# Attention with P on the array's columns: division once per head, two pairs with keys on partitions, scores by halves

## The chip, the cores and the metric

The kernel runs on one core of one Trainium2 chip. The core has a matrix engine (PE; PEld is its loading of the stationary operand, the weights), a vector engine (DVE), a scalar engine (ACT), a third elementwise engine (POOL), and a sync engine (SP), which here issues every DMA. SBUF is the on-chip working memory with 128 partitions; PSUM takes the results of matmuls in eight banks. The metric is the device time of one execution in microseconds. It is the median of several runs.

## The reference

Attention over 4 batches and 8 heads, 768 rows, 64 columns per head. A query sees only those keys that have the same six hash bits (the signs of six projections). The result of all heads goes through a gated MLP that also mixes along the sequence.

```python
q_bits = (einsum('bhsd,dk->bhsk', q, proj) > 0)      # 6 bits; the same for k
mask = q_bucket[:, :, :, None] == k_bucket[:, :, None, :]
scores = where(mask, q @ k.T / sqrt(64), -1e9)
scores = scores - max(scores, axis=-1)
attn = exp(scores); attn = attn / (sum(attn, axis=-1) + 1e-9)
x = concat_heads(attn @ v)                           # (4, 768, 512)
h = maximum(x @ w_in, 0); u, v = h[..., :512], h[..., 512:]
v_n = (v - mean(v)) / sqrt(var(v) + 1e-6)
v_s = einsum('ts,bsd->btd', w_spatial, v_n) + b_spatial[None, :, None]
out = (u * v_s) @ w_out
```

All inputs are float32. A row whose mask leaves no key at all gets the plain mean of v, because all its scores are equal.

## The kernel before, in words

**Numbers.** Every operand of a matmul is kept as two float16 parts, high and low, whose sum is the float32 value. A product is three matmuls: high times high, high times low, low times high. ACT usually makes the high part (a copy to float16), and DVE or POOL makes the low part (float32 minus high part).

**Pairs and rounds.** Two heads make a pair p (16 pairs, 4 per batch); head e of a pair sits on partitions 64e to 64e+63. A round is one block of 128 query rows of a pair, for both heads. There are six rounds per pair. In a round, `scores` does this:

- PE: for each head, 8 matmuls of 384 columns into two PSUM banks `sp` (three for the split product, one for the hash bits, whose large products push masked keys far down, for each half of the 768 keys). The two heads run on the two halves of the array's rows.
- DVE (L359): copies 128x768 scores to SBUF (`ex`), cuts them from below and takes each row's maximum (`mx`).
- POOL (L362): maximum times a negative factor (`nb`). ACT (L367): exp in place with bias `nb`, and the row sums (`sm`). POOL and DVE (L369, L370): the reciprocal `ri`.
- ACT (L373): high part of exp times `ri`. DVE (L375): the low part. Both lie in `pp`.
- SP: a transposing DMA turns `pp` into `pt`, with the keys on the partitions.

After three rounds, `weighted` multiplies: v (`vp`, high and low) is the stationary operand with 64 columns, `pt` streams 384 columns, and the two heads fill the two halves of the array's columns (36 matmuls into `pv`). The result is already the transposed attention output `xt`; ACT and DVE split it (L402, L405).

**Per pair.** SP loads k and q (`qk`) and v (`v32`); a hash product `hp` gives the signs (`sg`), which eight DMAs spread into `hr`; ACT and DVE split k and q (`hl`) and v (`vp`).

**MLP.** When the four pairs of a batch are done, `mlp` makes 28 units of PE work: six `v_unit` (vps), eight `u_unit` (ups), eight `s_unit` (sps, the mix along the sequence), six `o_unit` (ops, the output). Around them stand evacuations from PSUM, the normalisation, the gating product (POOL, `sy`) and splits of `vn` and `g` (ACT high, POOL low). In the order of the code a half batch is u, s, o.

**Weights.** `job` loads a piece of a weight matrix, brings the float64 words to float32 where needed (five small operations, four on DVE), and splits it: high on ACT, a second scaled copy on ACT, low on POOL.

**What sets the order.** All operations are recorded first with an engine, a cost and a key (the round in which they are due). `plan()` simulates the five engines with these costs, buffer rings and waits; whenever an engine is free, the ready operation with the smallest key goes next. The kernel is then written out in that order, and every engine executes its instructions strictly in it. So the costs, keys and ring sizes decide the order on each queue.

Of the kernel before, what the change touches and what calls it, by code (L numbers as in the profile page):

```python
# [6 lines left out]

F16 = mybir.dt.float16
F32 = mybir.dt.float32
I64 = mybir.dt.int64  # L10
U32 = mybir.dt.uint32
AF = mybir.ActivationFunctionType
ALU = mybir.AluOpType

P = 128
D = 64
# [7 lines left out]
SP = 16384.0  # L24
# [8 lines left out]
def lsh_attention_spatial_gating(  # L33
# [33 lines left out]


# [4 lines left out]
    for i, t in enumerate(hr):  # L73
        (nc.vector if i % 2 else nc.gpsimd).memset(t, 0.0)

# [8 lines left out]
    RING = {"sc": 2, "pv": 2, "m": 2, "hr": NHR, "qk": 1, "v32": 1, "hl": 2, "vp": 2, "sg0": 1, "sg1": 2,  # L84
            "ex": 6, "pp": 4, "pt": 4, "xt": 6, "st2": 4, "st6": 4, "v32m": 4, "vy": 2, "vn": 1, "u": 1,
            "g": 1, "sy": 2, "sm3": 2, "bs": 2, "mv": 2}
# [10 lines left out]
    unit = []  # L97

    def op(eng, dur, key, fn, r=(), w=(), kind=None, land=0.0):
        o = Op()  # L100
        o.eng, o.dur, o.key, o.fn, o.kind, o.land = eng, dur, key, fn, kind, land
        o.seq, o.new, o.start, o.end = len(ops), [], None, None
        deps = set()
        for x, wr in [(x, False) for x in r] + [(x, True) for x in w]:
# [4 lines left out]
            if wr and not b.users and b.tag is not None:  # L109
                o.new.append(b)  # L110
            b.uses.append((part, wr, o))
# [10 lines left out]
    def plan():  # L122


        SEM, MODE, DMA_LAT = 0.1, 0.1, 1.6
        LATE = {"PE": 0.17, "DVE": 0.09, "ACT": 0.1, "POOL": 0.05, "SP": 0.0}
# [8 lines left out]
        dma = 0.0  # L135
# [3 lines left out]
        def release(o):  # L139
            when[o] = max([d.end + (SEM if d.eng != o.eng or d.land else 0.03) for d in o.deps], default=0.0)  # L140
            ready[o.eng].append(o)

        def room(o):
            t = 0.0
            for b in o.new:
                ring = rings[b.tag]
                need = sum(1 for x in o.new[:o.new.index(b)] if x.tag == b.tag)
# [8 lines left out]
            return t  # L156

# [5 lines left out]
        while done < len(ops):  # L163
            nxt = None
            for e in free:
                while free[e] <= now:
                    best = None
                    for o in ready[e]:
# [3 lines left out]
                        t = max(t, when[o])  # L172
                        if t > now:
                            nxt = t if nxt is None else min(nxt, t)
                        elif best is None or (o.key, o.seq) < (best.key, best.seq):
                            best = o
# [3 lines left out]
                    ready[e].remove(o)  # L180
# [3 lines left out]
                    d = o.dur  # L184
# [4 lines left out]
                    free[e] = now + d  # L189
                    o.end = now + d + LATE[e]  # L190
# [14 lines left out]
        return sorted(ops, key=lambda o: (o.start, o.seq))  # L205

# [17 lines left out]
    def weights():  # L224
        vi, vo, vs = (x.rearrange("(c p) f -> p c f", p=P) for x in (w_in, w_out, w_sp))
        n = 0
        for src, dst, cs, lo, hi, m, f, W, key, dk in (
                (vi, wi, NPAIR, F2, DF, 256, SX, Wv, 5.0, 1.9), (vi, wi, NPAIR, 0, F2, 256, SX, Wu, 20.5, 1.0),
                (vs, ws, NT, 0, S, HS, SW, Ws, 28.0, 0.5), (vo, wo, NF, 0, DM, 256, SX, Wo, 33.5, 0.5)):
# [7 lines left out]
    def job(n, src, dst, m, f, W, key):  # L237
# [8 lines left out]
        else:  # L246
# [19 lines left out]
            for k, e, d in ((0, "ACT", 0.33), (4, "DVE", 0.2), (1, "DVE", 0.2), (2, "DVE", 0.34), (3, "DVE", 0.34)):  # L266
                op(e, d, key, lambda k=k: conv(k), r=[raw], w=[wb])
        d = 0.31 if m == 256 else 0.41
        op("ACT", d, key, lambda: nc.scalar.activation(dst[0], wb.t[:, :m], AF.Copy, scale=f), r=[wb], w=[(W, n)])
        op("ACT", d, key, lambda: nc.scalar.activation(wb.t[:, :m], wb.t[:, :m], AF.Copy, scale=f), w=[wb])  # L270
        op("POOL", 0.63 if m == 256 else 0.87, key,
           lambda: nc.gpsimd.tensor_tensor(out=dst[1], in0=wb.t[:, :m], in1=dst[0], op=ALU.subtract), r=[wb], w=[(W, n)])


    KH, KL, QH, QL = range(4)
    xts = {}

    def pair(p):
# [5 lines left out]
        def hash_():  # L284
# [7 lines left out]
        op("ACT", 0.42, k0 + 0.2, lambda: nc.scalar.activation(  # L292
            tile_of(s1, wk, [P, HS], F16, f"sg1_{p}"), s0.t, AF.Copy, scale=hv[:, 1:2]), r=[s0], w=[s1])
# [14 lines left out]
        def high():  # L308
            tile_of(hl, wk, [P, 4, S], F16, f"hl{p}")
            nc.scalar.activation(part(0), qk.t, AF.Copy, scale=SQ)  # L310

        op("ACT", 1.38, k0 + 0.5, high, r=[qk], w=[hl])
        op("DVE", 1.67, k0 + 0.6, lambda: nc.vector.scalar_tensor_tensor(
            out=part(1), in0=qk.t, scalar=SQ, in1=part(0), op0=ALU.mult, op1=ALU.subtract), r=[qk], w=[hl])
# [300 lines left out]
```

## Time and profile before

The median of three runs is 727.33 us (726.72 to 727.62). The profiled execution took 725.48 us, and its span, from the first to the last instruction, is 723.7 us; the mean granted clock of PE is 0.92.

| engine | busy us | share of the span | instructions |
|---|---|---|---|
| PE | 602.5 | 83% | 4352 |
| PEld | 302.6 | 42% | 4352 |
| DVE | 528.4 | 73% | 985 |
| ACT | 507.4 | 70% | 905 |
| POOL | 200.5 | 28% | 322 |

In the rows of a profile, `L214 PE MATMUL sp<-hl 64*128 64x384 f16 x1152 | 169.3, 374 | 82.6 <-DVE ex L359 79.7` reads: line 214, matmuls from tile hl into tile sp, 64 rows and 128 columns of the array, 64 partitions by 384 elements, 1152 of them; busy 169.3 us, 374 ns for one; PE was idle 82.6 us ahead of them, of which 79.7 until DVE had finished line 359 on tile ex. All matmuls have one line, that of a helper, so they are told apart by tiles. A row of the timeline or of the chain begins with the start and the duration in us. Records of matmuls are longer than the distance between them, because matmuls overlap in the array.

### The profile page before, as it was taken

The page shows a single profiled execution, that of the slowest core. Times are in us where ns is not written, and L with a number is a line of the kernel's source. Part 1 is how long each engine was busy: PE and PEld are TensorE (multiplying, and loading weights), DVE is VectorE, ACT ScalarE, POOL GpSimd, SP SyncE. Part 2 cuts the span into 40 slices and gives each one's busy share as a digit, 9 for nine tenths or more (in the row PEclk, how much of TensorE's full clock was granted, in tenths as well). Part 3 has the DMA queues.
Part 4 walks back from the last instruction along what each step waited for, and adds up shares of the span by engine and source line. Part 5 has one row for each costly group of instructions (what it writes and reads, how often), then busy time and mean ns, then how long its engine had stood idle before and what let it go on. Part 6 is the DMA issues. An engine that isn't in the chain of part 4 may idle for free. (4 is left out here: it accounts for less than half of the span.)

```text
span 723.7 us, 12276 instructions
## 1 busy us (share of the span) xinstructions
PE 602.5 (83%) x4352; PEld 302.6 (42%) x4352; DVE 528.4 (73%) x985; ACT 507.4 (70%) x905; POOL 200.5 (28%) x322
## 2 busy tenths in 40 slices
PE   2658566658888875999899989969998999989997
PEld 0224223333444432455344545534454555445553
DVE  3869788978799889857679876985788968864100
ACT  3768577878899768856777877785768778763221
POOL 2022122233144443106014420420033502302513
PEclk9998666666999985999999999989999999999999
DMA  4677988979798779886786869779856997790011
GB/s 137 178 160 155 223 178 159 224 142 236 124 237 150 176 166 217 186 177 138 135 202 126 171 126 217 162 152 181 159 112 139 178 178 131 146 202 3 1 45 43
DMA packets 317726, 111.73 MB, mean 154 GB/s; under 512 B 304224, under 2 KB 307296, under 8 KB 317664
## 3 DMA queue, kind: packets, MB, share of 16 engines
q1 hardware_dynamic: 317664, 110.94, 74.3%
q8 instruction: 34, 0.56, 0.3%
q14 instruction: 28, 0.23, 0.1%
HBM read 27.94 MB, written 6.29 MB: 47 GB/s over the span
## 5 line engine op out<-in xcount | busy, mean ns | idle before, releaser
L214 PE MATMUL sp<-hl 64*128 64x384 f16 x1152 | 169.3, 374 | 82.6 <-DVE ex L359 79.7
L375 DVE SCALAR_TENSOR_TENSOR pp<-ex,ri,pp 128x768 f16<-128x768 f32 x192 | 199.2, 1063 | 46.9 <-ACT pp L373 46.0
L373 ACT ACTIVATE pp<-ex,ri 128x768 f16<-128x768 f32 x192 | 172.3, 927 | 56.5 <-DMA pt<-pp 21.9
L367 ACT ACTIVATE ex<-ex,nb 128x768 f32<-128x768 f32 x192 | 177.5, 925 | 42.9 <-POOL nb L362 42.8
L359 DVE TENSOR_SCALAR_CACHE_REDUCE ex<-sp 128x768 f32<-128x768 f32 x192 | 179.2, 947 | 23.6 <-PE sp L214 23.3
L214 PEld LDWEIGHTS <-hl 64*128 64x128 f16 x1152 | 66.7, 103 | 171.0 <-issue 117.8
L214 PE MATMUL pv<-pt,vp 128*64 128x384 f16 x1152 | 112.7, 350 | 10.5 <-DMA pt<-pp 10.4
L214 PE MATMUL sps<-ws,vn 128*128 128x384 f16 x576 | 98.3, 328 | 0.0
L214 PE MATMUL sp<-hr 64*128 64x384 f16 x384 | 92.3, 376 | 4.1 <-DMA hr<-sg 4.1
L214 PEld LDWEIGHTS <-vp 128*64 128x64 f16 x1152 | 70.7, 118 | 54.6 <-issue 17.3
L369 POOL TENSOR_SCALAR ri<-sm 128x2 f32<-128x2 f32 x96 | 29.3, 305 | 199.6 <-ACT ex L367 192.8
L362 POOL TENSOR_SCALAR nb<-mx 128x2 f32<-128x2 f32 x96 | 37.0, 385 | 151.6 <-DVE ex L359 129.0
L214 PEld LDWEIGHTS <-vn 128*128 128x128 f16 x576 | 54.8, 98 | 41.9 <-issue 7.6
L214 PE MATMUL ops<-wo,g 128*128 128x512 f16 x288 | 66.9, 383 | 1.8 <-POOL g L520 1.0
L214 PE MATMUL ups<-xt,wi 128*128 128x384 f16 x384 | 66.0, 326 | 2.4 <-ACT vr L432 1.3
L214 PE MATMUL vps<-wi,xt 128*128 128x512 f16 x288 | 65.3, 380 | 0.6 <-ACT vr L432 0.5
L214 PEld LDWEIGHTS <-wi 128*128 128x128 f16 x384 | 36.4, 98 | 31.1 <-issue 8.0
L508 DVE SCALAR_TENSOR_TENSOR sy<-sps,bt 128x384 f32<-128x384 f32 x32 | 17.6, 551 | 42.3 <-PE sps L214 40.6
L511 POOL TENSOR_TENSOR sy<-sy,u 128x384 f32<-128x384 f32 x32 | 36.2, 1131 | 39.4 <-DVE sy L508 39.1
L471 POOL TENSOR_TENSOR vn<-vy,vn 128x512 f16<-128x512 f32 x24 | 31.3, 1313 | 48.0 <-ACT vn L468 47.9
L214 PEld LDWEIGHTS <-g 128*128 128x128 f16 x288 | 26.7, 98 | 40.0 <-issue 5.2
L214 PEld LDWEIGHTS <-xt 128*128 128x128 f16 x288 | 26.8, 98 | 37.0 <-issue 6.5
(49 smaller groups left out, 517.2 us busy)
## 6 DMA issues: line engine op xcount, KB each, us to landing
qk<-kq SPq DMA_DIRECT2D x16, 768.0 KB
v<-v SPq DMA_DIRECT2D x16, 384.0 KB
out<-o SPq DMA_DIRECT2D x24, 256.0 KB
raw<-w_in SPq DMA_DIRECT2D x16, 256.0 KB
pt<-pp SPq DMA_TRANSPOSE x192
raw<-w_sp SPq DMA_DIRECT2D x12, 192.0 KB
hr<-sg SPq DMA_DIRECT2D x128, 9.0 KB
raw<-w_out SPq DMA_DIRECT2D x8, 256.0 KB
```

Source lines behind the costliest of these rows:

```text
L214: nc.tensor.matmul(out_, lhsT=lhsT, rhs=rhs, start=start, stop=stop, **({} if pos is None else {"tile_position": pos}))
L359: nc.vector.tensor_scalar(tile_of(ex[e], wk, [P, 2, HS], F32, f"ex{p}_{i}_{e}"), ps[e].t[:, :, :HS], -float(2 ** 27), None, op0=ALU.max, o ...
L362: op("POOL", 0.25, g, lambda: nc.gpsimd.tensor_scalar(tile_of(nb, wk, [P, 2], F32, f"nb{p}_{i}"), mx.t, -ISQ, None, op0=ALU.mult), r=[mx], ...
L367: nc.scalar.activation(ex[e].t, ex[e].t, AF.Exp, bias=nb.t[:, e:e + 1], scale=ISQ, accum_out=sm.t[:, e:e + 1])
L369: op("POOL", 0.2, g, lambda: nc.gpsimd.tensor_scalar(tile_of(ri, wk, [P, 2], F32, f"ri{p}_{i}"), sm.t, 1e-9, 1.0 / SP, op0=ALU.add, op1=AL ...
L373: op("ACT", 0.83, g, lambda e=e: nc.scalar.activation(tile_of(pp[e], wk, [P, 2, 2, HS], F16, f"pp{p}_{i}_{e}")[:, 0], ex[e].t, AF.Copy, sc ...
L375: op("DVE", 0.93, g, lambda e=e: nc.vector.scalar_tensor_tensor(out=pp[e].t[:, 1], in0=ex[e].t, scalar=ri.t[:, e:e + 1], in1=pp[e].t[:, 0] ...
L471: op("POOL", 1.11, key, lambda i=i, y=y: nc.gpsimd.tensor_tensor(out=vn[1].t[:, i], in0=y.t, in1=vn[0].t[:, i], op=ALU.subtract), r=[y], w ...
L508: op("DVE", 0.47, key, lambda: nc.vector.scalar_tensor_tensor(out=tile_of(y, wk, [P, HS], F32, f"sy{b}_{d}_{h}"), in0=ps.t[:, :HS], scalar ...
L511: op("POOL", 0.96, key, lambda: nc.gpsimd.tensor_mul(y.t, y.t, u[h].t[:, d]), r=[(u[h], d)], w=[y])
```

## The change

**P is the stationary operand.** The weighted sum (now `sums`, in both `scores` and the new `scores_k`) loads 128 columns of `pt` as weights and streams v: 64 high columns and a column of ones (65) or 64 low columns. For each head and round there are 18 matmuls, with an array of full size. Both heads have a PSUM tile of six blocks of 65 columns for the whole pair, so the output has the queries on its partitions, and column 64 of each block is the sum of the row.

**Division once per head.** P is not divided any more: exp without row sums (L511), high part (`cast`, L244 on ACT or L246 on DVE), low part by plain subtraction (L515). `normalize` takes the reciprocal of the six row sums of a head, multiplies, splits the result (`xs`), and one transposing DMA per pair gives `xt`.

**Scores by halves.** A score product covers 384 keys and writes one bank per head; the ring of these banks has four entries. DVE cuts each half (L506) and joins the two maxima (L508, L509, formerly L362 on POOL).

**Two pairs with keys on partitions.** For pairs 2 and 3 `row_max` first computes all the scores of the pair roughly (high parts alone) to get the maxima (L410), transposes them on PE, and puts them by DMA into a row of `hr`, so that the score product itself subtracts them. `scores_k` then computes scores with keys on the partitions: exp straight from PSUM (L454), split, and no transposing DMA. `mean_v` and three more operations in `normalize` give the rows without keys their mean.

**Engines and order.** Some operations may run on one of two engines, and `plan()` picks (L515 and the splits of `xs` on DVE or POOL; casts on ACT or DVE). The planner treats DVE and POOL operations marked `lock` as exclusive. The low parts of weights are made on DVE in one operation, with weight jobs due 20 rounds earlier and with other keys. Evacuations of the MLP have keys 20 smaller, MLP keys are 6 larger, and a batch's units come as v, u0, s0, u1, o0, s1, o1.

```diff
-    RING = {"sc": 2, "pv": 2, "m": 2, "hr": NHR, ... "ex": 6, "pp": 4, "pt": 4, "xt": 6, ...
+    RING = {"sc": 4, "pv": 2, "m": 2, "hr": NHR, ... "ex": 5, "pp": 6, "pt": 4, "xt": 7, ...
...
+    KP = {2, 3}
...
+                op("DVE", 0.48, g + c / 4, cut, r=[ps[e]], w=[(ex[e], c), (mx, (e, c))])
+        op("DVE", 0.07, g, lambda: nc.vector.tensor_max(tile_of(nb, ...), mx.t[:, :, 0], mx.t[:, :, 1]), r=[mx], w=[nb])
+        op("DVE", 0.07, g, lambda: nc.vector.tensor_scalar(nb.t, nb.t, -ISQ, None, op0=ALU.mult), w=[nb])
...
+            op("ACT", 0.83, g, lambda e=e: nc.scalar.activation(ex[e].t, ex[e].t, AF.Exp, bias=nb.t[:, e:e + 1], scale=ISQ), r=[nb], w=[ex[e]])
...
+            op("ACT", 0.73, g, lambda eng, e=e: cast(
+                eng, tile_of(pp[e], ...)[:, 0], ex[e].t), r=[ex[e]], w=[pp[e]], alt=("DVE", 0.46))
+            op("DVE", 0.87, g, lambda eng, e=e: eng.tensor_tensor(out=pp[e].t[:, 1], in0=ex[e].t, in1=pp[e].t[:, 0], op=ALU.subtract),
+               r=[ex[e]], w=[pp[e]], lock=True, alt=("POOL", 1.6))
...
+                a = acc[e].t[:, :NT * 65].rearrange("p (a b) -> p a b", b=65)[:, i, :]
+                for c in range(NT):
+                    vl, vh = vp.t[:, 2 * c + e, 0:D], vp.t[:, 2 * c + e, D:2 * D + 1]
+                    mms.append((a, pt[e].t[:, c, :], vh, i == 0 and c == 0, False, None))
+                    mms.append((a[:, 0:D], pt[e].t[:, c, :], vl, False, False, None))
+                    mms.append((a, pt[e].t[:, NT + c, :], vh, False, i == NT - 1 and c == NT - 1, None))
+            op("PE", 0.54, g, sums, r=[pt[e], vp], w=[acc[e]], kind="w")
...
+    def row_max(p, hl, hrb):
+                        matmuls([(t[:, :HS], hl.t[r, QH, qs], hl.t[r, KH, cs], True, False, (D * e, 0)),
+                                 (t[:, :HS], hrb.t[z, 1, qs], hrb.t[z, 0, cs], False, True, (D * e, 0))])
+                        nc.vector.reduce_max(mh.t[:, e, i, c:c + 1], ps.t[:, :HS], axis=AX.X)
...
+    def scores_k(p, i, hl, hrb, mrow, vp, acc):
+                    nc.scalar.activation(ex[e].t[:, c], ps[e].t[:, :HS], AF.Exp, scale=ISQ)
...
-            op("PE", 1.95, key, product, r=[(x, h) for x in xt] + [Wu], w=[ps], kind="m")
+            op("PE", 1.95, key, product, r=xt + [Wu], w=[ps], kind="m")
...
+        units = [(v_unit, i) for i in range(NT)]
+        for k, (f, *a) in zip(keys, units + u0 + s0 + u1 + o0 + s1 + o1):
```

Three places of the built programs show what moves. First PE, at the first weighted sum of pair 0. Before (`vp` is v, `pt` the transposed P, the last figures are the output's partitions and columns):

```order
L214 LDWEIGHTS hr_74
L214 MATMUL sp_0_1_429<-hr_74 128x384
L214 LDWEIGHTS vp_104
L214 MATMUL pv_0_452<-pt_0_0_259,vp_104 64x384
L214 LDWEIGHTS vp_104
L214 MATMUL pv_0_452<-pt_0_1_270,vp_104 64x384
```

Now:

```order
L257 LDWEIGHTS hr_80
L257 MATMUL sp_3_1_1_313<-hr_80 128x384
L257 LDWEIGHTS pt_0_0_284
L257 MATMUL pv_0_338<-vp_101,pt_0_0_284 128x65
L257 LDWEIGHTS pt_0_0_284
L257 MATMUL pv_0_338<-vp_101,pt_0_0_284 128x64
L257 LDWEIGHTS pt_0_0_284
L257 MATMUL pv_0_338<-vp_101,pt_0_0_284 128x65
```

The weights are P now, each load is followed by a matmul of 65 or 64 columns instead of 384, and a slice of P's high part is loaded twice in a row.

Second POOL, at the end of pair 7 and in pair 8. Before (`nb`, `ri` are two numbers per row, `sy` and `g` belong to the MLP):

```order
L369 TENSOR_SCALAR ri7_2_3345<-sm7_2_3301 128x2
L362 TENSOR_SCALAR nb7_3_3428<-mx7_3_3407 128x2
L369 TENSOR_SCALAR ri7_3_3452<-sm7_3_3430 128x2
L362 TENSOR_SCALAR nb7_4_3508<-mx7_4_3470 128x2
L511 TENSOR_TENSOR sy0_0_1_3549<-sy0_0_1_3549,u0_1_3391 128x384
```

Now:

```order
L684 TENSOR_TENSOR g0_1_1_5206<-sy0_0_1_5140,g0_0_1_5205 128x384
L515 TENSOR_TENSOR pp8_2_0_5232<-ex8_2_0_5165,pp8_2_0_5232 128x768
L675 TENSOR_TENSOR sy0_1_1_5234<-sy0_1_1_5234,u0_1_4446 128x384
L565 TENSOR_TENSOR xs7_5286<-x7_0_5262,xs7_5286 128x6x64
L515 TENSOR_TENSOR pp8_2_1_5291<-ex8_2_1_5180,pp8_2_1_5291 128x768
```

POOL's tiny operations are gone, and between the products of the MLP stand subtractions of 768 elements: 164 of the 192 are on POOL.

Third DVE. Before, in pair 6 (`ex<-sp` is the cut, `pp<-ex,ri` the low part of P):

```order
L375 SCALAR_TENSOR_TENSOR pp6_0_0_2795<-ex6_0_0_2711,ri6_0_2786,pp6_0_0_2795 128x768
L375 SCALAR_TENSOR_TENSOR pp6_0_1_2829<-ex6_0_1_2719,ri6_0_2786,pp6_0_1_2829 128x768
L359 TENSOR_SCALAR ex6_2_0_2844,mx6_2_2843<-sp6_2_0_2809 128x768
L370 RECIPROCAL ri6_1_2847<-ri6_1_2847 128x2
L359 TENSOR_SCALAR ex6_2_1_2891,mx6_2_2843<-sp6_2_1_2810 128x768
```

Now, in pair 8:

```order
L506 TENSOR_SCALAR ex8_0_0_4994,mx8_0_4995<-sp8_0_0_1_4965 128x384
L506 TENSOR_SCALAR ex8_0_1_5000,mx8_0_4995<-sp8_0_1_1_4966 128x384
L508 TENSOR_TENSOR nb8_0_5023<-mx8_0_4995 128x2
L509 TENSOR_SCALAR nb8_0_5023<-nb8_0_5023 128x2
L506 TENSOR_SCALAR ex8_1_0_5060,mx8_1_5061<-sp8_1_0_0_5028 128x384
L246 CAST pp8_0_0_5073<-ex8_0_0_4994 128x768
```

DVE cuts halves, the two operations for `nb` stand between the halves of two rounds, and instead of two subtractions per round there is a cast in some rounds.

386 lines of the change are left out of this document (250 added, 136 removed), and 3 rows, old and new, of the table RING.

## Prediction

> **What bounds the kernel now.** I read busy time by stage first, then the matmuls in order of time, then the chain that ended last, then single groups. Columns of the stage view: stretch, length, busy time of PE, PEld, DVE, ACT and POOL (with instructions), granted clock, DMA share, GB/s.
>
> ```profile
> span 723.7 us, 12276 instructions
> 0.00:180.00 180.00, 110.78 (x742) 48.64 (x743) 137.47 (x268) 129.37 (x233) 42.54 (x77) 0.78 0.83 178
> 180.00:637.00 457.00, 413.50 (x3157) 212.06 (x3155) 368.38 (x674) 350.60 (x621) 135.26 (x220) 0.96 0.81 164
> 320.00:640.00 320.00, 300.67 (x2318) 155.38 (x2318) 255.07 (x458) 239.87 (x418) 90.00 (x152) 0.98 0.78 158
> 637.00:724.00 87.00, 78.22 (x458) 41.89 (x456) 22.54 (x47) 27.40 (x53) 22.68 (x25) 1.00 0.24 53
> ```
>
> The cuts are the first vps product and the last score:
>
> ```profile
> L214 PE MATMUL vps<-wi,xt x288: 376/379/390, 179.7 to 662.8; 128*128 128x512 f16 x144
> L214 PE MATMUL sp<-hr x384: 322/323/524, 13.1 to 636.7; 64*128 64x384 f16 x192
> ```
>
> Stage 1 (to 180) is batch 0's attention, with no MLP to fill PE. No engine is full: DVE 76%, DMA 0.83, PE 62% at clock 0.78. Stage 2 (180 to 637) holds 69 rounds of scores and nearly three MLPs; PE is busy 90% of it and 94% from 320 on, against 80% for DVE. There PE paces. Stage 3 (637 to 724) is almost all PE. Most of what PE loses from 320 to 640 is waiting for score buffers that DVE still reads:
>
> ```profile
> L214 PE MATMUL sp<-hl 64*128 64x384 f16 x588 | 69.8, 330 | 12.2 <-DVE ex L359 12.0
> L214 PE MATMUL pv<-pt,vp 128*64 128x384 f16 x603 | 55.2, 335 | 5.0 <-DMA pt<-pp 4.9
> ```
>
> So the sum is: stage 1, limited by everything but PE; PE's work in stage 2 over a busy share; PE's work in stage 3.
>
> **Prices on PE.** From the chain that ended last (start, length, what, count):
>
> ```profile
> 599.61 1.41 PE sp L214 x16
> 601.02 3.03 PE sps L214 x18
> 605.45 3.05 PE pv L214 x36
> 655.34 7.88 PE vps L214 x36
> 663.22 7.80 PE ups L214 x48
> 682.73 0.03 issue
> 686.05 5.57 PE ops L214 x25
> 720.02 0.03 ACTq L534
> ```
>
> A full-width matmul of 384 columns costs 7.80/48 = 0.1625 us, of 512 columns 0.219 (vps) to 0.223 (ops). Scores run in pairs on two row halves, pv in pairs on two column halves: 16 in 1.41 and 36 in 3.05 are 0.0813 each plus about 0.10 for entering another array shape. The timeline shows that 0.10: the pair of scores starts at 600.69 and the next product at 600.95, 0.26 later instead of 0.16.
>
> ```profile
> 600.69 0.33 PE L214 MATMUL sp<-hr 64*128 64x384 f16 x2
> 600.94 0.11 PEld L214 LDWEIGHTS <-vn 128*128 128x128 f16 x2 [0.32 <-issue]
> 600.95 0.50 PE L214 MATMUL sps<-ws,vn 128*128 128x384 f16 x2
> ```
>
> The new sum is 18 matmuls per head and 128 rows, 3456 in all, each with its own load of 128 weight columns and a stream of only 65 or 64. No row has so short a stream. Lower bound: 0.219/512 x 65 = 0.028 us, if every load hides. The row of two loads says how much a load can add: one lasts 98 ns, yet both are over in 0.11, so the second started some 15 ns behind the first, and the first product started 0.01 behind its own load. Load then stream, nothing hidden: 0.043. Far upper bound: 0.085, the whole 3.05/36 of pv, if a load and its matmul have a fixed price. I take **0.033**: in the long runs every load stands under the matmul ahead of it, and that is the near end.
>
> A rule speaks against this. The Trainium skill, "TensorE: Matmul & The Clock Gate", section "Back-to-back issue gap", gives about 81 ns per matmul for a stream of loads and 128-column matmuls. By it, as an estimate, stage 2 would come out some 127 us longer. No run here shows that figure; with 65 columns it lies close to the far bound, and the result is the second rival below.
>
> **Stage 1, part by part.** DVE's work, from these rows:
>
> ```profile
> L375 DVE SCALAR_TENSOR_TENSOR pp<-ex,ri,pp 128x768 f16<-128x768 f32 x192 | 199.2, 1063 | 46.9 <-ACT pp L373 46.0
> L359 DVE TENSOR_SCALAR_CACHE_REDUCE ex<-sp 128x768 f32<-128x768 f32 x192 | 179.2, 947 | 23.6 <-PE sp L214 23.3
> 332.45 0.95 DVE L359 TENSOR_SCALAR_CACHE_REDUCE ex<-sp 128x768 f32<-128x768 f32 x1
> 333.32 1.75 DVE L313 SCALAR_TENSOR_TENSOR hl<-qk,hl 128x1536 f16<-128x1536 f32 x1
> L262 DVE SCALAR_TENSOR_TENSOR w<-raw,w 128x256 uint32<-128x256 uint32 x24 | 11.2, 467 | 0.5
> L258 DVE TENSOR_SCALAR w<-w 128x256 f32<-128x256 f32 x24 | 7.2, 305 | 0.0
> ```
>
> From start to start a cut takes 0.87; 384 fewer elements at about 1.04 ns leave 0.47 for a half. Before vps the old order has 26 rounds, 52 cuts (45 us) and 48 subtractions (46). The new one has some 58 halves (27), 48 row maxima of 384 (like a half, 23), 8 subtractions (8), 12 casts (0.5 each by L258's rate: 6), 30 products for the low weights that POOL did (13), 4 more weight jobs (two ops like L262 and two like L258 each, 6 together), and about 50 tiny operations (6): 137.5 - 91 + 89 = **135**. DVE wins nothing. The gains lie beside it: pairs 2 and 3 need no transposes of P (24 of batch 0's 48 go, 4 of xt come), their exp reads PSUM directly, and ACT sheds the accumulator reads. I let DVE rise from 76% to 79%: **170 us**; unchanged share 177, and 155 if it reaches 87% as PE's neighbours do later. PE's 88 us of work at clock 0.78 fits under it.
>
> **Stage 2.** By the two orders, between the first vps and the last score (PE matmuls):
> - before: pv 828 x 0.0813 = 67.3; scores 1104 x 0.0813 = 89.8; MLP 212.5; hashes 7; 161 changes of shape at 0.10 = 16: 393 us of work. Its records are busy 413.5, a factor of 1.053.
> - after: sums 2412 x 0.033 = 79.6; scores 88.5; MLP 184.7 (of batch 2's MLP the last four s and all six o products, 72 matmuls each, now stand behind the last score); hashes 7; 212 changes = 21: 381 us, busy 401.
>
> A score now waits for a half buffer, so I take away half of the 12.0 us wait: of 19.3 us idle in 320 to 640 some 13 stay, a busy share of 0.958. Before 320 the old share is lower: its o products follow their s products with nothing of the MLP between, and the new order puts u products there. 401/0.958 = **419 us**; with the old 0.905 it would be 443.
>
> ACT has cover: per old round 2 x (0.925 + 0.188 + 0.927), per new one 2 x 0.925 and fewer than 2 casts. The 16 transposes of xt and 168 of P are fewer than 192. POOL is the new load. It takes 164 subtractions of 768 elements, priced by two uncontended groups of the last stage:
>
> ```profile
> L520 POOL TENSOR_TENSOR g<-sy,g 128x384 f16<-128x384 f32 x8 | 7.3, 911 | 5.0 <-ACT g L517 5.0
> L471 POOL TENSOR_TENSOR vn<-vy,vn 128x512 f16<-128x512 f32 x5 | 5.7, 1155 | 11.8 <-ACT vn L468 11.8
> L367 ACT ACTIVATE ex<-ex,nb 128x768 f32<-128x768 f32 x192 | 177.5, 925 | 42.9 <-POOL nb L362 42.8
> L367 ACT ACTIVATION_READ_ACCUMULATOR ex<-ex,nb 128x1 f32 x192 | 36.1, 188 | 0.0
> L373 ACT ACTIVATE pp<-ex,ri 128x768 f16<-128x768 f32 x192 | 172.3, 927 | 56.5 <-DMA pt<-pp 21.9
> ```
>
> 1.9 ns per element, so 1.64 us each, 269 us in all. That is costed at nothing in the sum; what it costs if the cover fails is the first rival.
>
> **Stage 3.** Behind the last score stand 144 sum matmuls (4.8), 144 ops (32.1), 216 sps (35.1), 96 ups (15.6), 72 vps (15.8) = 103.4. Of the two holes between s and o products (682.73 to 686.05) one is now covered by u products, 3.3 stays; 3.7 from 720.02 to the end. **110 us** against 87. The last pair's new chain (division, split, transpose of xt) hides under the 27 us of the previous MLP's products.
>
> 170 + 419 + 110 = 699 span. The median lies 3.6 over the profiled span (727.33 against 723.7): **703 us**, 3.3% faster. With stage 1 at 160 to 180 and 0.028 to 0.04 per matmul: 688 to 722.
>
> **Rivals.**
>
> *POOL and DVE block each other.* At 525 two subtractions on DVE, two on POOL and vy overlap:
>
> ```profile
> 525.32 2.84 DVE L375 SCALAR_TENSOR_TENSOR pp<-ex,ri,pp 128x768 f16<-128x768 f32 x2
> 525.75 3.42 POOL L471 TENSOR_TENSOR vn<-vy,vn 128x512 f16<-128x512 f32 x2 [2.67 <-ACT vn L468]
> 528.09 1.37 DVE L461 TENSOR_SCALAR vy<-vr,mv,rs 128x512 f32<-128x512 f32 x1
> L461 DVE TENSOR_SCALAR vy<-vr,mv,rs x24: 526/545/1374, 208.7 to 668.9; 128x512 f32<-128x512 f32 x24
> ```
>
> Alone they take 2 x 1.01, 2 x 1.155 and 0.545. They run one after the other. POOL would be on such work about 287 of stage 2's 419 us (123 of the subtractions, 202, and 85 for MLP and xt). A DVE operation on SBUF that meets one waits some 0.68 x 0.82 = 0.56 us. The two tiny ones at L508/L509 stand ahead of every exp, with the next round's halves queued behind them; with 1.6 others that is about 2.0 us per round on top of DVE's 4.3 (368.4 less 131 for subtractions, plus 57 for casts, tiny operations and the remaining ones). At 90% use 7.0 us per round, 68 rounds: 476, **760 us**. It decides once waits exceed some 1.2 us per round. For it: 269 us of new POOL work of just the kind that collides here. Against: many waits fall where DVE idles anyway.
>
> *Weight loads are not hidden*: 0.085 per matmul adds 2412 x 0.052 x 1.053/0.958 = 138 and 7 in stage 3: **848 us**. For it: nothing here shows short streams. Against: the two loads within 0.11.
>
> *The rounds keep their pace*: stage 1 stays at 180 and the busy share at 0.905: 180 + 443 + 110 + 4 = **737 us**, slower because stage 3 grew.
>
> *Everything hides*: 155, 0.028 and a share of 0.98: 155 + 397 + 110 + 4 = **666 us**.
>
> **Chances.** Forecast 0.56, all hidden 0.08, pace kept 0.13, POOL and DVE 0.17, loads 0.06. A measurement tells 0.2%, about 1.5 us, from no change. Faster: 0.54 of the forecast, 0.08 and 0.03 of the kept pace = 0.65; same 0.04 (the edges of these two); slower 0.31. The range 668 to 755 leaves out the loads, half of the block and half of all hidden, some 0.19 in all; the forecast alone is 688 to 722.
>
> **What would show it.** vps starts at 165 to 175. In a run of 18 pt matmuls the starts lie 30 to 36 ns apart; 80 or more means the second rival. In stage 2 PE is busy over 94%, and scores wait little for DVE. L508 and L509 at a mean near 0.16 us clear the first rival; 0.5 or more each, and exp waiting for nb, make it. Behind the last score 110 us. I am wrong if DVE, not PE, is the fullest engine of stage 2.

## The result, and the profile after

The changed kernel takes **776.6 us** (774.8 to 782.1 in four runs) against 727.0 (725.3 to 727.6): 1.070 times as long, 95% interval 1.064 to 1.076. The forecast was 703, the range 668 to 755. Some repeated runs of one kernel lie 3 to 7 us apart here, so single times below are read to about 5 us.

Stages of the profiled execution, in the columns of the prediction (PE, PEld, DVE, ACT, POOL, clock, DMA share, GB/s), cut at the first vps and the last score:

```profile
0.00:210.00 210.00, 132.06 (x1503) 71.74 (x1504) 170.46 (x379) 109.12 (x185) 104.65 (x85) 0.80 0.56 131
210.00:672.50 462.50, 404.92 (x4589) 231.64 (x4587) 386.76 (x996) 269.31 (x385) 279.77 (x204) 0.94 0.88 163
672.50:780.30 107.80, 102.49 (x672) 55.51 (x672) 25.64 (x59) 27.97 (x52) 38.00 (x36) 1.00 0.24 56
```

Forecast were 170, 419 and 110. Stage 3 is right; stage 1 is 40 us over and stage 2 is 43 over. PE is busy 88% of stage 2, not 95.8%: it has the work that was forecast (405 us against 401) and stands idle for the rest. The costliest groups that changed:

```profile
L515 POOL TENSOR_TENSOR pp<-ex,pp 128x768 f16<-128x768 f32 x148 | 251.5, 1714 | 175.4 <-DVE pp L246 87.2 <-ACT pp L244 58.6 <-DVE ex L506 8.5
L511 ACT ACTIVATE ex<-ex,nb 128x768 f32<-128x768 f32 x168 | 149.7, 927 | 135.7 <-DVE nb L509 131.7 <-DVE rv L547 3.9
L509 DVE TENSOR_SCALAR nb<-nb 128x2 f32<-128x2 f32 x84 | 63.0, 750 | 1.8
L508 DVE TENSOR_TENSOR nb<-mx 128x2 f32<-128x2 f32 x84 | 44.7, 532 | 1.9
L506 DVE TENSOR_SCALAR_CACHE_REDUCE ex<-sp 128x384 f32<-128x384 f32 x336 | 172.6, 548 | 31.9 <-PE sp L257 30.2 <-POOL pp L515 1.6
L301 DVE TENSOR_SCALAR w<-w 128x256 f32<-128x256 f32 x24 | 19.9, 833 | 1.2 <-ACT w L297 1.2
L307 DVE SCALAR_TENSOR_TENSOR w<-raw,w 128x256 uint32<-128x256 uint32 x24 | 18.4, 769 | 0.0
```

Two DVE operations on two elements per partition take 0.53 and 0.75 us, and exp waits 131.7 us for them. The weight operations at L301 and L307, 305 and 422 ns before (L258 and L264 there), take 833 and 769. The cut at L506, which reads PSUM, keeps its 0.55. The row of before for L264:

```profile
L264 DVE SCALAR_TENSOR_TENSOR w<-raw,w 128x256 uint32<-128x256 uint32 x24 | 10.1, 422 | 0.3
```

The timeline of stage 2 of the change shows one such wait (start, length, engine; DVE's, then POOL's, then ACT's rows):

```profile
583.92 0.56 DVE L506 TENSOR_SCALAR_CACHE_REDUCE ex<-sp 128x384 f32<-128x384 f32 x1
584.51 0.16 DVE L508 TENSOR_TENSOR nb<-mx 128x2 f32<-128x2 f32 x1
584.71 1.56 DVE L509 TENSOR_SCALAR nb<-nb 128x2 f32<-128x2 f32 x1
583.00 3.24 POOL L515 TENSOR_TENSOR pp<-ex,pp 128x768 f16<-128x768 f32 x2 [3.22 <-DVE mv L603]
586.37 0.94 ACT L511 ACTIVATE ex<-ex,nb 128x768 f32<-128x768 f32 x1 [3.50 <-DVE nb L509]
```

POOL's two subtractions end at 586.24. L509 "runs" until 586.27, though 0.16 is its length when nothing is in its way; ACT's exp starts 0.1 later, after 3.50 us of idling. A wait of this kind is no gap on DVE: it stands inside the instruction's own time, so DVE looks busy.

The same trace shows that this holds throughout. Of the 84 instances of L509, the 34 that overlap no two-input POOL operation take 165 ns on average and 171 at most; the 50 that do take 1147. For L508 it is 152 ns for 23 and 675 for 61, for L301 285 ns for 12 and 1380 for 12. Of the 168 instances of L508 and L509, 81 last over 0.5 us, and each of these ends 0.01 to 0.08 us behind the end of a POOL operation. The cut takes 548 ns beside POOL and 550 without.

### The profile page after: what moved, and what is told of

It reads as the page before. It is cut to its first block, busy times and chain, and to the rows that moved or that the text cites. A ratio compares the mean times of both kernels' runs of the same rounds, so it can differ in the third digit from the quotient of the medians.

```text
span 780.3 us, 17339 instructions
## 1 busy us (share of the span) xinstructions
PE 639.5 (82%) x6758; PEld 358.9 (46%) x6758; DVE 582.9 (75%) x1429; ACT 406.4 (52%) x621; POOL 422.4 (54%) x325
## 4 chain that ended last, share of the span: by engine, by line
PE 38%; DVE 28%; DMA 12%; issue 8%; ACT 5%; POOL 5%; SPq 4%; POOLq 0%; ACTq 0%; DVEq 0%
PE sps L257 9%; PE sp L257 8%; DVE ex L506 8%; DMA pt<-pp 8%; PE pv L257 6%; PE ups L257 5%; PE ops L257 4%; PE vps L257 4%; SPq L341 3%; DVE nb L509 3%; ACT ex L511 3%; DVE nb L508 2%; POOL pp L515 2%; DVE mh L410 2%; DMA qk<-kq 2%
## 5 line engine op out<-in xcount | busy, mean ns | idle before, releaser
L515 POOL TENSOR_TENSOR pp<-ex,pp 128x768 f16<-128x768 f32 x148 | 251.5, 1714 | 175.4 <-DVE pp L246 87.2
L511 ACT ACTIVATE ex<-ex,nb 128x768 f32<-128x768 f32 x168 | 149.7, 927 | 135.7 <-DVE nb L509 131.7
L506 DVE TENSOR_SCALAR_CACHE_REDUCE ex<-sp 128x384 f32<-128x384 f32 x336 | 172.6, 548 | 31.9 <-PE sp L257 30.2
L257 PE MATMUL pv<-vp,pt 128*128 128x65 f16 x3024 | 126.3, 200 | 53.3 <-DMA pt<-pp 51.8
L257 PEld LDWEIGHTS <-pt 128*128 128x128 f16 x3024 | 112.5, 101 | 97.8 <-DMA pt<-pp 69.1
L257 PE MATMUL sp<-hr 63*128 63x384 f16 (+1 forms) x384 | 81.6, 359 | 10.2 <-DMA hr<-mt 6.0
L244 ACT ACTIVATE pp<-ex 128x768 f16<-128x768 f32 x108 | 87.8, 831 | 0.7
L509 DVE TENSOR_SCALAR nb<-nb 128x2 f32<-128x2 f32 x84 | 63.0, 750 | 1.8
L246 DVE CAST pp<-ex 128x768 f16<-128x768 f32 x60 | 38.3, 638 | 21.6 <-ACT ex L511 21.1
L257 PEld LDWEIGHTS <-hr 63*128 63x128 f16 (+1 forms) x432 | 30.6, 104 | 48.5 <-issue 35.2
L508 DVE TENSOR_TENSOR nb<-mx 128x2 f32<-128x2 f32 x84 | 44.7, 532 | 1.9
## 6 DMA issues: line engine op xcount, KB each, us to landing
qk<-kq SPq DMA_DIRECT2D x16, 768.0 KB
```

What stands on the lines that cost most here:

```text
L244: eng.activation(out_, in_, AF.Copy, scale=1.0 if scale is None else scale)
L246: eng.tensor_copy(out_, in_)
L257: nc.tensor.matmul(out_, lhsT=lhsT, rhs=rhs, start=start, stop=stop, **({} if pos is None else {"tile_position": pos}))
L506: nc.vector.tensor_scalar(ex[e].t[:, c], ps[e].t[:, :HS], -float(2 ** 27), None, op0=ALU.max, op1=ALU.max, accum_out=mx.t[:, e, c:c + 1])
L508: op("DVE", 0.07, g, lambda: nc.vector.tensor_max(tile_of(nb, wk, [P, 2], F32, f"nb{p}_{i}"), mx.t[:, :, 0], mx.t[:, :, 1]), r=[mx], w=[nb])
L509: op("DVE", 0.07, g, lambda: nc.vector.tensor_scalar(nb.t, nb.t, -ISQ, None, op0=ALU.mult), w=[nb])
```

## The experiments

Times are of one run each, beside a run of the kernel before on the same chip (727.8 for e and g, 731.2 for f, 728.3 for h and k); the last two kernels are medians of four runs, beside 729.7. The edits below are abridged to what differs. Two marks are used beside the stages: the start of the 25th round of scores (all of batch 0's rounds are then issued), found by counting the scores' matmuls in order of time, 16 to a round, and the start of the first vps.

| kernel | time | 25th round | first vps | last score |
|---|---|---|---|---|
| before | 727 | 164 | 180 | 637 |
| the change | 777 | 180 | 210 | 672 |
| exp bias on ACT (e1) | 751 | 176 | 213 | 640 |
| no subtraction on POOL (e2) | 787 | 199 | 221 | 686 |
| no keys on partitions (e3) | 793 | 173 | 218 | 683 |
| old due times of weights (e4) | 792 | 158 | 189 | 681 |
| e1 + half the subtractions (f1) | 742 | 184 | 204 | 636 |
| e1 + none on POOL (f2) | 765 | 196 | 216 | 664 |
| e1 + MLP due early (f3) | 766 | 173 | 209 | 670 |
| f1 + MLP due early (f4) | 763 | 183 | 202 | 665 |
| e1 + half, from round 25 on (g1) | 745 | 175 | 212 | 632 |
| g1 + later weights (g2) | 744 | 173 | 211 | 637 |
| g1 + low parts on POOL (g3) | 766 | 175 | 209 | 658 |
| g1 + both (g4) | 756 | 177 | 211 | 646 |
| the change without conversion (k1) | 756 | 162 | 191 | 645 |
| the change, two products of three (k2) | 781 | 179 | 208 | 672 |
| f1 + old due times (h1) | 745 | 153 | 166 | 635 |
| f1 + w_sp, w_out later (h2) | 768 | 186 | 204 | 661 |
| f1 + pulled 6 rounds (m1) | 748 | 166 | 183 | 639 |
| f1 + earlier, not pulled (m2) | 751 | 171 | 187 | 641 |

### Which wait, and whose

The exp bias leaves the two operations that wait:

```
-op("DVE", nb = tensor_max(mx[:, :, 0], mx[:, :, 1]))
-op("DVE", nb = tensor_scalar(nb, -ISQ, mult))
+op("DVE", nb = reduce_max(mx, axis=X))
+op("ACT", nb = activation(nb, Copy, scale=-ISQ))
```

> The two tiny DVE operations ahead of each exp (L508, a maximum of two columns, and L509, a product in place) become one DVE row maximum over the pair of columns and one ACT product. Theory (POOL and DVE block each other, and the two tiny operations pay it ahead of exp): the wait of exp for DVE's nb falls from 131.7 us to under 70, a round of stage 2 loses 0.6 to 1.0 us, stage 2 goes from 462 to 395-420 us, the whole to 715-735 us. Rival (the transposes of P and the order of the engines set the pace, and the tiny operations only use up time that is idle anyway): 765-780 us, and the wait of exp moves to another releaser. If the new row maximum is stretched like the old pair (0.5 us or more), the wait is not about which tiny operation it is.

Measured: 750.6 us, 26 less. Groups and stages:

```profile
L508 DVE TENSOR_REDUCE nb<-mx 128x2 f32<-128x4 f32 x84 | 12.8, 153 | 1.8
L509 ACT ACTIVATE nb<-nb 128x2 f32<-128x2 f32 x84 | 16.7, 198 | 73.3 <-DVE nb L508 72.7
L511 ACT ACTIVATE ex<-ex,nb 128x768 f32<-128x768 f32 x168 | 150.0, 927 | 4.8 <-ACT nb L509 0.4
0.00:213.00 213.00, 137.50 (x1591) 75.31 (x1592) 172.53 (x416) 124.22 (x221) 100.82 (x85) 0.82 0.63 143
213.00:640.50 427.50, 387.48 (x4496) 225.97 (x4496) 304.88 (x879) 267.24 (x428) 286.25 (x204) 0.95 0.92 169
503.35 0.92 POOL L565 TENSOR_TENSOR xs<-x,xs 128x384 f16<-128x384 f32 x1
503.81 0.16 DVE L508 TENSOR_REDUCE nb<-mx 128x2 f32<-128x4 f32 x1
```

The two maxima per row, found by a reduction, take 153 ns, also in the middle of a POOL operation (503.81 against 503.35 to 504.27): 64 of the 84 overlap one, and none of these lasts over 159 ns. ACT waited 131.7 us ahead of exp; now 72.7 ahead of its product. DVE's busy time in the first two stages falls from 557 to 477 us with nothing taken away but one tiny operation of two per round. So the mechanism is the first rival's, but its size was over-rated: over the 96 rounds up to the last score a round loses 0.33 us (672 to 640), not 0.6 to 1.0, and the whole misses the expected 715 to 735. Stage 2 is 7 us over its expected 420, although it holds 65 rounds of scores where the change has 68; stage 1 did not move, and PE now waits 57.9 us for pt (51.8 in the change). The Trainium skill, "SBUF — State Buffer", section "Who interferes with whom", says that a DVE operation with two SBUF inputs, or a tensor_scalar in its fast mode, takes a port pair that GpSimd also needs, one of the two blocking the other for a whole instruction, and that a reduction never does. The rows agree: 532 and 750 ns for the first two kinds, 153 for the third. No run tells in which mode L509 ran.

Next, POOL's part itself (the alternative engine is removed, for L515 and L459):

```
-op("DVE", 0.87, g, subtract P's high part, lock=True, alt=("POOL", 1.6))
+op("DVE", 0.87, g, subtract P's high part, lock=True, alt=None)
```

> No subtraction of P goes to POOL: all 192 run on DVE. Theory (blocking): L509 and L508 fall from 750 and 532 ns to under 200, the weight operations L301 and L307 from 833 and 769 ns to about 305 and 422, and POOL's work of 278 us costs DVE some 155 us of its own; DVE is then the fullest engine of stage 2 with 420-440 us and the whole stays at 770-800 us. Rival (DVE's tiny operations are slow by themselves, POOL has no part in it): L509 stays above 0.5 us, and DVE's stage 2 grows past 480 us, the whole past 820.

Measured: 787.4 us.

```profile
L515 DVE TENSOR_TENSOR pp<-ex,pp 128x768 f16<-128x768 f32 x168 | 167.3, 1021 | 4.6 <-ACT pp L244 4.3
L508 DVE TENSOR_TENSOR nb<-mx 128x2 f32<-128x2 f32 x84 | 21.3, 253 | 0.4
L509 DVE TENSOR_SCALAR nb<-nb 128x2 f32<-128x2 f32 x84 | 18.1, 216 | 0.4
L301 DVE TENSOR_SCALAR w<-w 128x256 f32<-128x256 f32 x24 | 6.8, 281 | 3.3 <-ACT w L297 3.3
```

The tiny operations (216 and 253 ns) and the weights' (281) lose nearly all of their stretch: it was POOL. DVE is busy 403 us of stage 2, less than the 420 to 440 expected. Yet the kernel is 11 us slower, since DVE has the subtractions. Moving them to POOL was a gain, only a small one, and the marks place it: without them the 25th round starts 18 us later (199 against 180), and what follows takes 587 us instead of 600. Next, the same with the exp bias on ACT, together with an even split (the planner's weight for POOL 1.0 instead of 0.6: 80 of 192 there), and with the MLP due 2 rounds behind its batch (the first edit is in f1 and f4, the second in f3 and f4):

```
-WEIGH = {"DVE": 1.8, "ACT": 1.0, "POOL": 0.6}
+WEIGH = {"DVE": 1.8, "ACT": 1.0, "POOL": 1.0}
-keys = [NT * NPAIR * (b + 1) + 8.0 + n * 24.0 / 28.0 ...]
+keys = [NT * NPAIR * (b + 1) + 2.0 + n * 24.0 / 28.0 ...]
```

> As the run with the exp bias on ACT (750.6 us), and the planner's weight for POOL goes from 0.6 to 1.0, which leaves 80 of the 192 subtractions of P there instead of 162. Theory (what is left of the loss is still POOL and DVE serving one another's operations on SBUF in turn, above all the weight conversion in stage 1): the weight operations L301 and L307 fall from 437 and 656 ns towards 305 and 422, pair 4's scores start before 170 us instead of at 176, the whole is 728-742 us. Rival (the transposes of P, whose DMA share is 0.92 in that run's stage 2, hold it now): within 6 us of 750, PE's wait for pt stays near 58 us.

> As the run with the exp bias on ACT, and no subtraction of P on POOL. Theory (POOL's subtractions cost DVE as much waiting as they save it work): 745-760 us, that is the 162 subtractions moved to POOL are worth under 10 us once exp no longer waits. Rival (POOL's work is a real relief, and only the two tiny operations paid for it): DVE is the fullest engine of both stages and the whole is 765-790 us.

> As the run with the exp bias on ACT, and the MLP's products are due 2 rounds behind their batch again, not 8. Theory (the later due time leaves PE idle in stage 1 and its work behind the last score): the first vps starts 15 to 25 us sooner, what stands behind the last score falls from 108 to 85-95 us, the whole to 730-742 us. Rival (batch 0's attention and the weights set the first vps, and PE's work in stage 2 only grows by what leaves stage 3): 745-755 us.

> All three: exp bias on ACT, about half the subtractions on POOL, MLP due 2 rounds behind its batch. If the gains of the two runs before add: 710-728 us, level with or below the kernel before. If they are one gain told twice: 728-742.

Measured: 742.2, 765.1, 765.5 and 762.6. With none on POOL the loss against e1 is 14 us (11 if each is measured from the kernel before on its own chip), so the relief is real, and more than the theory gave it. But it is all in batch 0: the 25th round starts 20 us later than in e1 (196 against 176), and what follows takes 567 us against 573. The split is the best version found; its stages and weight rows:

```profile
0.00:204.00 204.00, 129.79 (x1473) 71.36 (x1474) 172.32 (x436) 116.16 (x210) 52.54 (x52) 0.79 0.58 140
204.00:636.00 432.00, 393.77 (x4662) 230.48 (x4660) 346.37 (x972) 270.83 (x427) 187.42 (x143) 0.96 0.94 173
L301 DVE TENSOR_SCALAR w<-w 128x256 f32<-128x256 f32 x24 | 8.7, 366 | 6.7 <-ACT w L297 6.7
L307 DVE SCALAR_TENSOR_TENSOR w<-raw,w 128x256 uint32<-128x256 uint32 x24 | 9.9, 414 | 0.0
```

From the 25th round to its end it takes 556 us, against 560 in the kernel before and 573 in e1; but the 25th round starts 8 us later than in e1, since DVE now has more subtractions in batch 0. The wait of PE for pt, 57.0 us, is no less than the 57.9 of e1, as its rival said. ACT even waits longer for nb than in e1 (106.4 us against 72.7) in a kernel that is faster, so the sum of one engine's waits is not the price of them. The early MLP was a clear miss: its first vps starts only 4 us sooner than in e1, what stands behind the last score falls from 108 to 94 us, but the last score comes 29 us later, twice what left the end. So moving PE's work ahead cost more than it saved; why, no run shows.

### What sets stage 2

The sum said that PE's work paces it. One of the three products of the sums is left out, in the same order:

```
 mms.append((a, pt[e].t[:, c, :], vh, ...))
-mms.append((a[:, 0:D], pt[e].t[:, c, :], vl, False, False, None))
 mms.append((a, pt[e].t[:, NT + c, :], vh, ...))
```

> The changed kernel in its own order, without the product of the high part of P with the low part of V for the 14 pairs with queries on partitions (1008 of the 3024 short matmuls; the output loses precision). If the chain over DVE, POOL and ACT sets the pace of stage 2: the whole falls by less than 12 us. If PE does: by 1008 x 0.036 = 36 us, less what falls on stage 1, so 25-36 us. A fall of 60 us or more would mean that a short matmul costs far more than its 0.036 us in the chain.

Measured: 780.6 us, no change. Stage 2 and exp's wait:

```profile
210.00:672.00 462.00, 386.80 (x3773) 208.80 (x3771) 381.13 (x987) 267.07 (x381) 277.20 (x203) 0.93 0.88 162
L511 ACT ACTIVATE ex<-ex,nb 128x768 f32<-128x768 f32 x168 | 149.7, 927 | 137.0 <-DVE nb L509 130.3 <-DVE rv L546 3.9 <-POOL vp L359 2.6
```

PE is busy 18 us less in a stage that is just as long, so PE's work does not pace it. That leaves the chain over DVE, POOL and ACT, whose waits e1 shortened, and the transposes of P, which no run took away. At this pace the price of a short matmul, on which the prediction spent most care, did not matter.

### What delays batch 0

Two parts were undone alone: the pairs with keys on partitions (`KP = set()`), and the weights' due times (the old table, and `key` for `key - 20.0`):

> No pair has its keys on partitions (that part of the change undone). Rival for the late stage 1 (the row maxima with their waits, and the sums that follow one another, make it late): stage 1 goes from 210 to 185-195 us, the whole to 755-765 us. Theory (weight work that was pulled ahead blocks ACT and the DMA queue): stage 1 stays at 205-215, the whole at 770-785 us.

> The weights' conversion has its old due times again (20 rounds later, and the old table). Theory (weight work pulled ahead holds up ACT in its order, waiting for raw weights from the DMA): ACT's 20.2 us of waiting for the raw w_sp blocks goes, stage 1 goes from 210 to 180-195 us, the whole to 745-765 us. Rival (stage 1 is late by the blocking of POOL and DVE): stage 1 stays within 5 us of 210 and the whole at 770-785 us.

Measured: 793.5 and 792.1, both slower than any expectation allowed. Without keys on partitions the 25th round starts 7 us sooner, but the rest takes 19 us more. Pairs 2 and 3 belong to batch 0, so how much of the 19 us is theirs and how much the planner's new order is not separated. With the old due times the first vps comes at 189, as expected, the 25th round at 158 instead of 180, and then all is lost again, and more: the last score comes at 681. To take the weights' DVE work away without moving anything, the four operations at L301 to L307 are left out in the change's own order (the MLP then works on other weights):

```
-op(e, d, key - 20.0, lambda k=k: conv(k), ...)
+op(e, d, key - 20.0, lambda k=k: conv(k) if k == 0 else None, ...)
```

> The changed kernel in its own order, without the four DVE operations that put a 64-bit weight together (L301 to L307; w_in and w_out are then the absolute value of one half of each word, so that the MLP works on other numbers; nothing else is left out). Theory (the weights' work on DVE, stretched by POOL and pulled ahead of the attention, makes stage 1 late): these 96 operations take 66 us, 53 of them in stage 1; the first 24 rounds end at 140-155 us instead of 180, the first vps starts at 170-182 instead of 210. Rival (the raw weights' DMA, the transposes and the row maxima set stage 1, and DVE has room for the rest): the first 24 rounds end at 168-180, the first vps at 200-210.

Measured: 755.6 us; the 25th round at 162, the first vps at 191. The gain, 18 us in batch 0, lies between the two expectations. Stage 1 of the change has 28 rounds, so the forecast put the 25th at 170 x 24/28 = 146 us, and the weights account for about half of the 34 us by which it came later.

```profile
0.00:180.00 180.00, 120.91 (x1438) 67.32 (x1440) 125.72 (x286) 103.85 (x179) 95.53 (x79) 0.82 0.63 148
POOL pp L515 <- DVE pp L246: 33.9, 6, 15.8
ACT ex L511 <- DVE nb L509: 19.5, 8, 5.4
ACT ws L244 <- DMA raw<-w_sp: 19.1, 4, 9.6
```

Without them DVE is busy only 70% there, so it isn't one full engine that holds the rest. Among the waits left in the first 190 us (time, number, longest) are: POOL for casts, exp for nb, and ACT 19.1 us for raw weights, with the attention's work behind them in ACT's order. What each of them is worth was not separated.

Eight versions then tried to have both, a short batch 0 and the 556 us behind it (g1 to g4 start from e1):

```
g1  {**WEIGH, "POOL": 1.0} if o.key >= 24 else WEIGH
g2  g1, w_sp due at 30 and w_out at 36 (24 and 29), w_in nearly by the old table
g3  g1, low parts: product on ACT, subtraction on POOL, as before the change
g4  g2 and g3
h1  f1, the old table and no "- 20.0"
h2  f1, w_sp due at 32 and w_out at 38, these without "- 20.0"
m1  f1, the old table, "- 6.0" for "- 20.0"
m2  f1, due at 5, 17, 22 and 28, no "- 20.0"
```

> As the run with the exp bias on ACT, and POOL's weight is 0.6 for the first 24 rounds and 1.0 after: many subtractions on POOL in stage 1, about half in stage 2. Theory (stage 1 is limited by DVE's work, stage 2 by the waits of POOL and DVE on one another and by PE): stage 1 keeps the pace of the first run, 6.9 us per round, stage 2 that of the run with half the subtractions, 6.3; with 31 and 65 rounds and 104 us behind them 730-736 us. Rival (the two runs differ by the order that the planner finds, not by the share of POOL): anywhere from 742 to 760 us.

> As the late half, and the weights are fetched and converted later (w_sp 6 and w_out 7 rounds later, w_in spread as before). Theory (the weight operations, some 60 us of DVE in stage 1, make it late): stage 1 loses 8 to 15 us, the whole is 718-728 us. Rival (the weights are then late for the first MLP, as in the run with the old due times): 735-760 us.

> As the late half, and the low parts of the weights are subtracted on POOL again, with a product on ACT ahead, as in the kernel before. Theory (DVE's own work limits stage 1): DVE sheds 17 us there, stage 1 loses 6 to 12 us, the whole is 722-730 us. Rival (POOL's operation makes DVE wait for as long as it saves): within 4 us of the late half.

> Late half, later weights and low parts on POOL together: if the gains add, 712-724 us, under the kernel before; if the weights come too late for the first MLP, 735-760 us.

> Exp bias on ACT, half the subtractions on POOL, and the weights with the due times of the kernel before (no 20 rounds ahead). If the gains add (the first 24 rounds end at 158 us as in the run with these due times alone, and the rest takes 556 us as in the run with half the subtractions): 718-728 us. If the weights, late, hold up the first MLP again: 735-755 us.

> As the run with half the subtractions on POOL (742 us), but w_sp and w_out are fetched 8 to 9 rounds later and are not pulled ahead; w_in as in the change. If the weights' work is what delays stage 1, a third of it leaves: the first 24 rounds end some 10 us sooner and the whole is 728-735 us; if not, 740-750 us.

> Exp bias on ACT, half the subtractions on POOL, and the weights' old due times with their work pulled only 6 rounds ahead, so that the first MLP's products stand in the order from round 27 (vps), 31 (ups) and 37 (sps), 10 rounds sooner for sps than in the run with the old due times. Theory (the weights' place is what ties the pace of batch 0's attention to the start of the first MLP, and neither end is right): the first 24 rounds end at 158-168 us, the rest takes 556-565, the whole is 716-735 us against 727 of the kernel before. Rival (DVE's total work up to the first MLP is the limit, wherever the weights stand): 738-750 us.

> As the run between, with due times 4 to 6 rounds sooner and no pull at all (vps from round 27, ups 31, sps 38 in the order). By the theory 718-735 us, by the rival 738-750 us; the two runs differ by under 8 us.

Measured: 745.3, 743.6, 765.7, 756.2, 745.0, 768.0, and as medians of four 748.1 (ratio to before 1.026, interval 1.021 to 1.031) and 750.5 (1.029, 1.025 to 1.034). None beats the kernel before, and every expectation of a gain fell. Low parts on POOL cost 20 us against g1 and batch 0 got nothing for it. In h1 the 25th round starts at 153, the earliest of all and 11 us ahead of the kernel before; but the weights of the first MLP's s products come late, its first sps starts at 287 us (264 in f1, 237 before), and its products later stand in one block on PE, while DVE's busy share falls from 57% to 36%:

```profile
360.00:375.00 15.00, 15.00 (x139) 8.82 (x138) 8.62 (x16) 6.43 (x10) 2.80 (x4) 0.93 1.14 243
375.00:390.00 15.00, 15.00 (x159) 8.52 (x158) 7.14 (x19) 5.25 (x9) 5.00 (x6) 1.00 0.73 124
390.00:405.00 15.00, 15.00 (x137) 7.86 (x136) 5.43 (x14) 5.75 (x10) 1.64 (x1) 1.00 0.75 161
```

m1 has its first sps at 262, as f1, but its 25th round starts at 166 and the rest takes 581 us:

```profile
0.00:183.00 183.00, 118.88 (x1455) 66.20 (x1456) 142.05 (x366) 102.73 (x181) 68.17 (x63) 0.83 0.60 138
183.00:641.00 458.00, 405.04 (x4677) 234.31 (x4676) 371.88 (x1027) 283.18 (x456) 201.51 (x152) 0.95 0.91 171
```

So what batch 0 gains is lost behind it, wherever the weights stand: these eight end between 744 and 768 us. f1, at 742, is 11 us behind the kernel before on its own chip and the best three of them (g1, g2, h1) 16 to 18, a lead of about the 5 us of a single run. **Open** stays what ties the two together. No engine is full in stage 2 of f1 (PE 91%, DVE 80%, DMA share 0.94), and its DMA share is the highest resource there; no run thinned out the transposes in that version, so that this is a guess. Each of these edits also makes the planner place everything else anew, and differences of some us between them may be that alone; only k1 and k2 kept the order.

## Why the prediction was wrong, point by point

**The step that failed first** is the one on POOL: "1.9 ns per element, so 1.64 us each, 269 us in all. That is costed at nothing in the sum". The price per operation was right (1714 ns, 1.64 when nothing is in its way), the cost was not. The rows at 525 us that the prediction quoted showed the blocking (though not quite "one after the other": alone these operations take 4.9 us, together 4.1), and it had worked out its result as the first rival: DVE slowed by some 2.0 us per round, stage 2 at 476 us, decided at waits of 1.2 us per round. Measured in stage 2 of the change:

```profile
L509 DVE TENSOR_SCALAR nb<-nb 128x2 f32<-128x2 f32 x69 | 54.0, 783 | 1.7
L508 DVE TENSOR_TENSOR nb<-mx 128x2 f32<-128x2 f32 x69 | 40.0, 580 | 1.7
```

Together they take 94 us of DVE, 1.36 us per round in place of 0.32, and stage 2 is 462. The overlaps in the trace, e1 and e2 show the cause from three sides. The rival that came true was given 0.17, against 0.56 for the sum. Its 760 us fell short by 17 through two errors that partly offset each other: stage 2 was 14 us shorter than its 476, stage 1 40 us longer than the 170 it kept. The argument against it, "many waits fall where DVE idles anyway", does not hold for an operation on which exp waits at once: it had no slack. The size is smaller than the miss, though: of the 74 us between forecast and result, freeing the exp bias (e1) gives back 26, and f1, which adds the even split, 34. What f1 still lacks, 39 us, lies nearly all in stage 1 (204 us against 170), and no run shows its cause.

**PE paces stage 2** ("401/0.958 = 419"). PE's work was right, 405. The share was carried over from the kernel before, where DVE had 20% to spare; with the waits it had 16%, most of it spent waiting for scores and for what is behind exp, and k2 shows that PE's work there could shrink by 18 us for nothing. With the two operations' waits gone stage 2 is 428 us (e1), near the forecast, but in part by luck: it holds 65 rounds and not 68, 6.6 us each where the forecast had 6.2.

**Stage 1** ("135", "170 us"): DVE was busy 170 us for 28 rounds. Groups of that stretch, columns as before:

```profile
L301 DVE TENSOR_SCALAR w<-w 128x256 f32<-128x256 f32 x18 | 17.0, 948 | 0.8 <-ACT w L297 0.8
L307 DVE SCALAR_TENSOR_TENSOR w<-raw,w 128x256 uint32<-128x256 uint32 x18 | 14.4, 807 | 0.0
L305 DVE SCALAR_TENSOR_TENSOR w<-raw,w 128x256 uint32<-128x256 uint32 x18 | 12.1, 678 | 0.1
L303 DVE TENSOR_SCALAR w<-w 128x256 uint32<-128x256 uint32 x18 | 9.2, 514 | 0.0
L313 DVE SCALAR_TENSOR_TENSOR ws<-raw,ws 128x384 f16<-128x384 f32 x12 | 9.9, 827 | 14.5 <-ACT ws L244 14.5
L313 DVE SCALAR_TENSOR_TENSOR wi<-w,wi 128x256 f16<-128x256 f32 x16 | 9.2, 575 | 0.0
```

The weights take 72 us where the sum had 42 (16 old jobs at 23, plus 13 and 6), which is most of the 35 us by which DVE's "135" was too small. By the means of e2 for L301, L303, L305 and L307 (281, 281, 413, 441) and for L313 (612 and 414) the same operations would be 40: the count was near (18 jobs and 28 products for 20 and 30), the 32 us are the blocking again, which the sum left out and the rival put only into stage 2. That "DVE rises to 79%" held (81%). But k1 says that DVE's work is not all of it: 53 us less of it gave 18. The forecast had no term for the in-order waits of ACT and POOL in batch 0.

**Right**: stage 3 (108 against 110), and the short matmul. The chain of the last stage, start, length, what, count:

```profile
682.56 1.09 PE pv L257 x36
686.58 0.55 PE pv L257 x18
705.36 15.54 PE vps L257 x72
720.89 7.80 PE ups L257 x48
```

1.09/36 is 0.030 us per load and matmul of 65 columns, in the forecast's interval and near the value taken, 0.033. That refutes the second rival (0.085); the 81 ns of the Trainium skill, "TensorE: Matmul & The Clock Gate", section "Back-to-back issue gap", for 128 columns does not carry over to 65. The third rival (pace kept, 737) and the fourth (all hidden, 666) did not happen. Of the signs named ahead, vps at 165 to 175, PE over 94% and L508/L509 near 0.16 all failed; "0.5 or more each, and exp waiting for nb" came as written. "DVE, not PE, is the fullest engine" did not: DVE 84%, PE 88% in stage 2, and still PE did not pace. Being the fullest is not being the bound.

Taken together, against the kernel before (profiled 723.7 and 780.3): 30 us in stage 1, 5.5 in stage 2 with less MLP work in it, 21 in stage 3, to which that work was moved.

## What to carry to other kernels

When work goes to POOL "for free", list the DVE operations on SBUF that will run beside it and ask of each what waits for it at once; two elements per partition are enough to hold up a chain, and they need a form that reads PSUM or reduces, or another engine. A busy share carried over from the old profile says which engine is fullest, not which one paces: leaving out some of its work in an unchanged order tells that in one run. And where one stage is limited by waits in the queues, moving work out of it is no gain until the stage that gets it has been priced as well.

## What the runs showed that was not expected

- A DVE operation that waits for POOL is recorded as running: 1.56 us for one of 0.16, ending 0.03 us behind POOL's (584.71). A mean per group of 750 ns for two columns is the only sign on the page of the profile.
- On the same buffer a row maximum of 128x4 kept 153 ns while a tensor_tensor and a tensor_scalar of 128x2 took 532 and 750 on average.
- Subtractions on POOL paid in batch 0 and cost behind it: without them (f2 against e1, each in its own order) the 25th round comes 20 us later and the rest is 6 us shorter.
- Loads of 128 columns hide nearly entirely under streams of 65: 36 pairs in 1.09 us, 30 ns each against the prediction's lower bound of 28, although one load by itself is recorded with 97 ns.
- Removing 1008 short matmuls, a third of those in 14 of 16 pairs, shortened nothing: 780.6 against 776.6 us.
